# First attention unit: merged key and query loads, a split first decay load, half-size scaling and score passes, and a new queue order

## The chip, the cores and the metric

One Trainium2 chip, one of its cores. The metric is the device time of one launch in microseconds (us), lower is better; each figure is the median of several runs, and the profile is of one further execution.

## The reference

Four sequences of 768 steps and eight heads of width 48 run through a decayed linear attention; its output, 3072 tokens of width 384, goes through two feed-forward layers.

```python
for t in range(S):
    state = alpha[:, :, t, :, None] * state + einsum('bhd,bhe->bhde', k[:, :, t], v[:, :, t])
    y[:, :, t] = einsum('bhd,bhde->bhe', q[:, :, t], state)
...
h = x @ w_in;  x = (h * cos(h)) @ w_out                                   # 384 -> 2048 -> 384
h = maximum(maximum(x @ w1, x @ w2), x @ w3);  return h @ w_out           # 384 -> 768 -> 384
```

## The kernel before

The tokens are cut into 6 units of 512 columns (4 sequences of 128 steps). A unit's attention is done for pairs of heads, on 128 partitions; the first layer then takes 16 steps per unit (`moe1`: L763 to L765 into the hidden block, L794 to L796 out of it), 96 steps in all; the second layer (L1147 to L1149, L1056 to L1058) follows. The attention of units 1 to 5 (`prepare`, `turn`, `visit`) is slipped between the steps of the unit before. All weights of the first layer arrive once as 64-bit numbers, in 32 blocks (`weight`): a load (L386), an upper part on ScalarE (L387), a merge on VectorE (L388), a high half on ScalarE (L392) and a low half on GpSimd (L396) or VectorE (L394).

Unit 0 has nothing to hide behind; it is `first_unit`. Three wide head pairs k = 0, 1, 2 carry a fourth one in their spare partitions. For each k:

- `load0` (L445) issues the loads, all on SyncE's queue: decays `al` (128 rows of 522 numbers), keys and queries `kq` in two loads of 512 numbers a row, then the values `v` and `rest`.
- `chain0` (L461): VectorE forms backward products of the decays in two scans (L471), each over two sequences; GpSimd multiplies the keys by them (L473); ScalarE makes a copy of the scaled keys for the shared fourth pair (L474); VectorE forms the forward products (two reciprocals L477, two scans L478); GpSimd multiplies the queries by these (L480).
- `scores0` (L489) and `shared_scores0` (L501) are passes of 8 small matmuls on TensorE (16 in the trace: a float32 matmul counts twice), `mask0` (L435) takes a score block out of PSUM through VectorE, `values0` (L517) and `shared_values0` (L526) multiply by the values, `transposes0` (L547) and `state0` (L567) form the state for unit 1, `outputs0` hands unit 0 to `moe1`.

The order on every queue comes from a planner in the kernel (`Program.order`): each operation has an engine, a cost, a due time and what it reads and writes; a simulated clock picks, for the engine that is free first, the ready operation with the smallest due time. The numbers at the head of the file (`W1E` sets how early a weight block is due, `LATE` and `LATE_S` the transposes and states of unit 0, `ATT0`, `VIS` and their like the visits, `B_START` and `B_STEP` the weights of the second layer) are due times or offsets of such. What waits for what on the chip is set by semaphores, so the planner's clock decides only the order.

```python
for n, (key, f, b) in enumerate((alpha(0), keys(0, 0), alpha(1), keys(0, 1), keys(1, 0), alpha(2), keys(1, 1), keys(2, 0), keys(2, 1), vals(0), vals(1), vals(2), shared_vals())):
    op("SP", HW, f, (), [key], -40 + 0.1 * n, 0.95 * dma(b) if n else 0)
```

Of the kernel before, what the change touches and what calls it, by code (L numbers as in the profile page):

```python
# [60 lines left out]
B_START, B_STEP = 17.76, 2.27  # L61
# [8 lines left out]
GLE1, GLQ = 0, 15  # L70
GLP1 = 0
# [7 lines left out]
GATE, GSTEP = 0, 3  # L79
LGATE = 11  # L80
W0 = -0.9
LATE, LATE_S = -3.58, -4.98
LOD = (1, 3)

W1E = 21
MOE_EARLY = 5
EARLY = 3
FIRST = -4
ATT0 = 3.97
ATTS = 3.25  # L90
# [189 lines left out]
SLOW = 1.2  # L280
# [16 lines left out]
def tile_kernel(ctx, tc, aa, qk, vv, vr, wt, outT):  # L297
# [147 lines left out]
    def load0():  # L445
        def alpha(k):
            return ("inf", k), lambda: nc.sync.dma_start(al_f[k], aa[0, k, :, 0:KO]), P * KO * 4

        def keys(k, h):
            return ("inq" if h else "ink", k), lambda: nc.sync.dma_start(kq_f[k][:, HB * h:HB * (h + 1)], qk[0, k, :, HB * h:HB * (h + 1)]), P * HB * 4  # L450

        def vals(k):
            return ("v", k), lambda: nc.sync.dma_start(v_b[k], vv[0, k]), P * HB * 3

        def shared_vals():
            return "vr", lambda: nc.sync.dma_start(rest, vr.rearrange("p (i j k e) -> p i j k e", i=N2, j=2, e=32)), P * N2 * 2 * NT0 * 128

        for n, (key, f, b) in enumerate((alpha(0), keys(0, 0), alpha(1), keys(0, 1), keys(1, 0), alpha(2), keys(1, 1), keys(2, 0), keys(2, 1), vals(0), vals(1), vals(2), shared_vals())):
            op("SP", HW, f, (), [key], -40 + 0.1 * n, 0.95 * dma(b) if n else 0)

    def chain0(k):  # L461
        t, gf, kg = al_f[k], g_f[k % NGS], ("g", k % NGS)
        g = gf[:, 0:AP].rearrange("p (c t) -> p c t", c=N2)
        fv = t[:, 0:AP].rearrange("p (c t) -> p c t", c=N2)
        kv3, qv3 = views0(k)
        kf, kk, kq, ka = ("inf", k), ("ink", k), ("inq", k), ("acc", 2)
        t0 = -30 + k
        ones, seeds = acc[2][:, 0:AP // 2], acc[2][:, HB - AP // 2:][:, ::-1]
        for h in range(2):
            hs = slice(AP // 2 * h, AP // 2 * (h + 1))  # L470
            op("DVE", 0.07 + 0.00208 * AP / 2, lambda hs=hs: ve.tensor_tensor_scan(  # L471
                gf[:, 0:AP][:, ::-1][:, hs], t[:, 1:AP + 1][:, ::-1][:, hs], ones, 0.0, ALU.mult, ALU.add), [ka, kf, *([("scan", k - 1)] if k else [])], [(*kg, h)], t0)
        op("Pool", pool(HB), lambda: ge.tensor_tensor(kv3, kv3, g[:, :, 1:], ALU.mult), [(*kg, 0), (*kg, 1)], [kk], t0)  # L473
        op("Act", act(HB), lambda: se.activation(kr_b[k], kq_f[k][:, 0:HB], AF.Copy, scale=shared), [kk, "shared"], [krk[k]], t0)  # L474
        for h in range(2):
            hs, cs = slice(AP // 2 * h, AP // 2 * (h + 1)), slice(N2 // 2 * h, N2 // 2 * (h + 1))
            op("DVE", 0.15, lambda cs=cs: ve.reciprocal(seeds[:, ::CP], g[:, cs, 0]), [ka, (*kg, 1 - h)], ["seeds"], t0)  # L477
            op("DVE", 0.07 + 0.00208 * AP / 2, lambda hs=hs: ve.tensor_tensor_scan(  # L478
                t[:, hs], t[:, hs], seeds, 0.0, ALU.mult, ALU.add), [ka, "seeds", (*kg, 0), (*kg, 1)], [kf, ("scan", k)], t0)
        op("Pool", pool(HB), lambda: ge.tensor_tensor(qv3, qv3, fv[:, :, 1:], ALU.mult), [kf], [kq], t0)  # L480

    def scores0(k, n, t):
        rk, r = psum2("r0")
        kv3, qv3 = views0(k)

        def amm():
            for i in range(N2):
# [3 lines left out]
        op("PE", SLOW * 0.95, amm, [("ink", k), ("inq", k)], rk, t, tiled=True, count=32)  # L491
        return mask0(n, r, rk, t + 0.01)

    def shared_scores0(n, t):
        rk, r = psum2("r0")

        def amm(k):
            kr3, qv3 = kr_b[k].rearrange("p (c t) -> p c t", c=N2), views0(k)[1]
            for i in range(N2):
                for j in range(2):  # L500
                    pe.matmul(r[j][:, i * P:(i + 1) * P], kr3[wide_half[j], i], qv3[wide_half[j], i],  # L501
                              start=(not k and not i), stop=(k == NT0 - 1), skip_group_check=True)
# [38 lines left out]
    def transposes0(k, t):  # L541
# [7 lines left out]
        op("PE", SLOW * N2 * 0.085, trans, [("ink", k), "ident", ("y1", LGATE)], [pk_k], t, count=2 * N2)  # L549
# [56 lines left out]
    def prepare(n, t0):  # L606
# [8 lines left out]
        op("SP", HW, lambda: nc.sync.dma_start(al_f[na], aa[u, p, :, 0:KO]), (), [kf], t0 - 4.8 + (0.8 if not k else 0), dma(PR * KO * 4), tiled=True)  # L615
        op("SP", HW, lambda: nc.sync.dma_start(kq_f[nk], qk[u, p]), (), [kk, kq], t0 - 3.9, dma(PR * 2 * HB * 4), tiled=True)
# [819 lines left out]
```

## Time and profile before

| what | us |
|---|---|
| median of 3 runs | 739.33 (738.73 to 739.82) |
| the profiled execution | 738.83 |
| its span, first to last instruction | 736.9 |
| TensorE busy | 730.0, 99% of the span |
| VectorE, ScalarE, GpSimd busy | 539.7, 420.1, 303.8 |
| DMA, share of 16 engines | 47.4% |

The engines are named PE (TensorE), DVE (VectorE), ACT (ScalarE), POOL (GpSimd), SP (SyncE, which issues the loads). The ends of matmuls are modelled, so a group's length is best read from its start to the start of the next group. The clock that was granted to TensorE is 1.00 of full speed in every slice.

### The profile page before, as it was taken

How to read it: one execution, taken by the hardware profiler on the slowest of the kernel's cores; microseconds unless marked ns; L12 is line 12 of the kernel's file. 1: busy time of each engine (PE TensorE's matmuls, PEld its weight loads, DVE VectorE, ACT ScalarE, POOL GpSimd, SP SyncE). 2: the span in 40 equal slices, each digit the busy share in tenths (PEclk: the TensorE clock that was granted, in tenths of full speed). 3: DMA queues.
4: the chain of work that ended last, by engine and by line, in shares of the span. 5: the costliest groups of instructions: out<-in, count | busy, mean ns of one | idle time of the engine just before them, and what ended most of it. 6: DMA issues, size and time to landing. Idle time of an engine off the chain costs nothing.

```text
span 736.9 us, 14861 instructions
## 1 busy us (share of the span) xinstructions
PE 730.0 (99%) x5815; PEld 600.8 (82%) x5815; DVE 539.7 (73%) x858; ACT 420.1 (57%) x801; POOL 303.8 (41%) x284
## 2 busy tenths in 40 slices
PE   8999999999999999999999999999999999999997
PEld 6788888888888888888888888888888888888886
DVE  7999996877877776865655666467787768677763
ACT  4888866666756666667644655443563345634233
POOL 6444433556533635454320211043465543614442
PEclk9999999999999999999999999999999999999999
DMA  8866534564644554554250111397625556246302
GB/s 319 298 226 212 171 126 134 176 222 158 206 139 154 187 181 136 184 180 148 98 207 0 44 43 44 140 368 292 213 103 201 198 177 205 77 149 206 130 1 85
DMA packets 47525, 120.41 MB, mean 163 GB/s; under 512 B 4736, under 2 KB 19968, under 8 KB 42464
## 3 DMA queue, kind: packets, MB, share of 16 engines
q1 hardware_dynamic: 47456, 119.48, 47.4%
q8 instruction: 45, 0.74, 0.4%
q14 instruction: 24, 0.20, 0.1%
HBM read 91.54 MB, written 25.95 MB: 159 GB/s over the span
## 4 chain that ended last, share of the span: by engine, by line
PE 96%; DVE 1%; ACT 1%; DMA 1%; issue 0%; SPq 0%; POOL 0%; DVEq 0%; POOLq 0%
PE acc L794 9%; PE ps L763 9%; PE acc L795 9%; PE acc L796 9%; PE ps L764 9%; PE ps L765 9%; PE ps L1147 6%; PE ps L1148 6%; PE ps L1149 6%; PE acc L1148 3%; PE acc L1147 3%; PE acc L1149 3%; PE acc L1057 2%; PE acc L1058 2%; PE acc L1056 2%; PE ps L662 2%
## 5 line engine op out<-in xcount | busy, mean ns | idle before, releaser
L763 PE MATMUL ps<-xt,wih 128*128 128x512 f32 x288 | 114.5, 397 | 0.0
L794 PE MATMUL acc<-gg,woh 128*128 128x512 f32 x288 | 114.4, 397 | 0.0
L796 PE MATMUL acc<-gg,woh 128*128 128x512 f32 x288 | 112.3, 390 | 0.2 <-DVE gg L789 0.2
L795 PE MATMUL acc<-gg,wol 128*128 128x512 f32 x288 | 112.2, 390 | 0.0
L764 PE MATMUL ps<-xt,wih 128*128 128x512 f32 x288 | 112.2, 390 | 0.0
L765 PE MATMUL ps<-xt,wil 128*128 128x512 f32 x288 | 112.2, 389 | 0.0
L772 DVE SCALAR_TENSOR_TENSOR q<-q,ps 128x512 f32<-128x512 int32 x96 | 65.5, 683 | 39.7 <-ACT q L771 39.2
L773 ACT ACTIVATE q<-q 128x512 f32<-128x512 f32 x96 | 60.4, 631 | 39.4 <-DVE q L772 39.2
L777 DVE TENSOR_TENSOR gg<-q,gg 128x512 fp32r<-128x512 f32 x81 | 62.8, 779 | 23.2 <-ACT gg L776 22.6
L771 ACT ACTIVATE q<-ps 128x512 int32<-128x512 f32 x96 | 56.9, 593 | 39.4 <-PE ps L765 37.4
L775 DVE TENSOR_TENSOR q<-q,ps 128x512 f32<-128x512 f32 x81 | 55.2, 681 | 33.0 <-ACT q L773 32.3
L776 ACT ACTIVATE gg<-q 128x512 fp32r<-128x512 f32 x81 | 51.1, 631 | 35.5 <-DVE q L775 31.1
L937 POOL TENSOR_TENSOR ar<-ar,ar 128x512 f32<-128x512 f32 x21 | 28.6, 1365 | 92.1 <-DVE as L946 67.8
L796 PEld LDWEIGHTS acc<-gg,woh 128*128 128x128 f32 x288 | 54.1, 188 | 12.1 <-DVE gg L789 0.8
L794 PEld LDWEIGHTS acc<-gg,woh 128*128 128x128 f32 x288 | 54.0, 188 | 11.8
L765 PEld LDWEIGHTS ps<-xt,wil 128*128 128x128 f32 x288 | 54.1, 188 | 11.3
L763 PEld LDWEIGHTS ps<-xt,wih 128*128 128x128 f32 x288 | 54.1, 188 | 11.1
L795 PEld LDWEIGHTS acc<-gg,wol 128*128 128x128 f32 x288 | 54.1, 188 | 10.4
L764 PEld LDWEIGHTS ps<-xt,wih 128*128 128x128 f32 x288 | 54.1, 188 | 10.4
L1155 ACT ACTIVATE q<-acc 128x512 f32<-128x512 f32 x36 | 21.5, 597 | 69.2 <-PE acc L1149 68.5
L1166 POOL TENSOR_TENSOR xf<-q 128x512 f32<-128x512 f32 x18 | 24.5, 1364 | 81.4 <-ACT q L1155 81.4
L1019 ACT ACTIVATE fs<-x 128x512 fp32r<-128x512 f32 x42 | 26.2, 630 | 44.8 <-DVE x L1170 30.0
(187 smaller groups left out, 1727.1 us busy)
## 6 DMA issues: line engine op xcount, KB each, us to landing
bs<-bfd SPq DMA_DIRECT2D x36, 1024.0 KB, 5.0
raw<-in_wt SPq DMA_DIRECT2D x56, 384.0 KB, 3.9
bfd<-bs SPq DMA_DIRECT2D x32, 384.0 KB, 2.9
kq<-in_qk SPq DMA_DIRECT2D x20, 512.0 KB, 4.4
al<-in_aa SPq DMA_DIRECT2D x23, 261.0 KB, 2.8
x1r<-yy SPq DMA_DIRECT2D x18, 256.0 KB, 2.1
ar<-x1r SPq DMA_DIRECT2D x18, 256.0 KB, 2.9
v<-in_vv SPq DMA_DIRECT2D x23, 192.0 KB, 4.5
```

The costliest lines, as they stand in the source:

```text
L763: pe.matmul(ps, wi["h"][:, f, cc], xt[:, cc, 0], start=(cc == 0), stop=False)
L764: pe.matmul(ps, wi["h"][:, f, cc], xt[:, cc, 1], start=False, stop=False)
L765: pe.matmul(ps, wi["l"][:, f, cc], xt[:, cc, 0], start=False, stop=(cc == NR - 1))
L772: op("DVE", dve(HB), lambda: ve.scalar_tensor_tensor(q, q.bitcast(I32), -TWOPI, ps, ALU.mult, ALU.add), [hk], [qk], m)
L773: op("Act", act(HB), lambda: se.activation(q, q, AF.Sin, bias=0.5 * math.pi), (), [qk], m)
L777: op("DVE", dve(HB), lambda: ve.tensor_tensor(gl, q, gh.bitcast(F32), ALU.subtract), [qk, ("gh", gn)], [("gl", gn)], m, port=True)
L794: pe.matmul(acc[c], oh, gh, start=(f == 0), stop=False)
L795: pe.matmul(acc[c], ol, gh, start=False, stop=False)
L796: pe.matmul(acc[c], oh, gl, start=False, stop=(f == NF1 - 1))
L1147: pe.matmul(bank, bt[:, i, 0], at[:, 0], start=start, stop=False, skip_group_check=skip)
L1148: pe.matmul(bank, bt[:, i, 0], at[:, 1], start=False, stop=False, skip_group_check=skip)
L1149: pe.matmul(bank, bt[:, i, 1], at[:, 0], start=False, stop=stop, skip_group_check=skip)
```

## The change

`load0` loads keys and queries of a pair in one transfer, and the first decays in two (columns 258 to 521 first, then 0 to 257). `chain0` scales the keys of pair 0 and the queries of all three pairs in halves of two sequences, and each score pass of the unit is cut into two halves that wait for their half alone. The numbers that set due times are new, and `GLP1` gives the low half of step 0 of the first layer to GpSimd.

```diff
-B_START, B_STEP = 17.76, 2.27
+B_START, B_STEP = 31.64, 2.16
...
-GLE1, GLQ = 0, 15
-GLP1 = 0
+GLE1, GLQ = 0, 16
+GLP1 = 1
...
-GATE, GSTEP = 0, 3
-LGATE = 11
+GATE, GSTEP = 1, 0
+LGATE = 14
...
-LATE, LATE_S = -3.58, -4.98
+LATE, LATE_S = -4.18, -2.37
...
-W1E = 21
-MOE_EARLY = 5
+W1E = 37
+MOE_EARLY = 6
...
-ATT0 = 3.97
-ATTS = 3.25
-VIS, VEND, VQ = 3.95, 12, 0.98
-LARGE, STALL, PATIENT = 2, -0.53, 2.75
-V2, V2S, TA = 16.24, 2.98, 0.97
+HALF_K, HALF_Q, SPLIT0 = (0,), (0, 1, 2), True
+ATT0 = 4.42
+ATTS = 1.66
+VIS, VEND, VQ = 4.24, 13, 0.53
+LARGE, STALL, PATIENT = 2, -1.22, 8.27
+V2, V2S, TA = 17.49, 2.63, 1.77
...
-SLOW = 1.2
+SLOW = 1.06
...
+        def keys(k):
+            return [("ink", k), ("inq", k)], lambda: nc.sync.dma_start(kq_f[k], qk[0, k])
...
+        first = [(0.1, 0.0, [("infb", 0)], alpha(0, cut, KO)), (0.4, 0.0, [("inf", 0)], alpha(0, 0, cut))] if SPLIT0 else [(HW, 0.0, [("inf", 0)], alpha(0))]
...
+        if k in HALF_K:
+            for h in (1, 0):
+                cs = halves0[h][1]
+                op("Pool", pool(HB // 2), lambda cs=cs: ge.tensor_tensor(kv3[:, cs], kv3[:, cs], g[:, cs, 1:], ALU.mult), [(*kg, 1 - h), kk], [("kp", k, h)], t0)
...
-        op("Pool", pool(HB), lambda: ge.tensor_tensor(qv3, qv3, fv[:, :, 1:], ALU.mult), [kf], [kq], t0)
+        if k in HALF_Q:
+            for h in range(2):
+                cs = halves0[h][1]
+                op("Pool", pool(HB // 2), lambda cs=cs: ge.tensor_tensor(qv3[:, cs], qv3[:, cs], fv[:, cs, 1:], ALU.mult), [("f0", k, h), kq], [("qp", k, h)], t0)
...
+    def score_parts(k, go, keys, rk, t):
+        parts = ((0, 1), (2, 3)) if k in HALF_Q else ((0, 1, 2, 3),)
+        for p in parts:
+            hs = sorted({i // 2 for i in p})
+            op("PE", SLOW * 0.95 * len(p) / 4, lambda p=p: go(p), [*(x for h in hs for x in (*keys(h), *queries0(k, h)))], rk, t, tiled=True, count=8 * len(p))
```

What that does to the order stands below, at three places. In the names, `al_124` to `al_126` are the decays of pairs 0 to 2, `kq_104` to `kq_106` their keys and queries, `g_127` and `g_128` backward products of pairs 0 and 1, `raw_88` to `raw_91` four buffers of weight blocks, `inv_122` a buffer that is zeroed for unit 1.

SP's queue from the first load, before:

```order
L447 DMA al_124<-in_aa 128x522
L450 DMA kq_104<-in_qk 128x512
L447 DMA al_125<-in_aa 128x522
L450 DMA kq_104<-in_qk 128x512
L450 DMA kq_105<-in_qk 128x512
```

and in the changed kernel:

```order
L450 DMA al_124<-in_aa 128x264
L387 DMA raw_88<-in_wt 128x1536
L450 DMA al_124<-in_aa 128x258
L453 DMA kq_104<-in_qk 128x1024
L450 DMA al_125<-in_aa 128x522
L453 DMA kq_105<-in_qk 128x1024
```

A weight block (128 rows of 1536 two-byte numbers) now goes second, between the two parts of the first decays; before, the first weight block was behind all 13 loads of the unit.

POOL from its first product, before:

```order
L473 TENSOR_TENSOR kq_104<-kq_104,g_127 128x512
L480 TENSOR_TENSOR kq_104<-kq_104,al_124 128x512
L473 TENSOR_TENSOR kq_105<-kq_105,g_128 128x512
L480 TENSOR_TENSOR kq_105<-kq_105,al_125 128x512
```

and in the changed kernel:

```order
L480 TENSOR_TENSOR kq_104<-kq_104,g_127 128x256 x2
L493 TENSOR_TENSOR kq_104<-kq_104,al_124 128x256 x2
L483 TENSOR_TENSOR kq_105<-kq_105,g_128 128x512
L397 TENSOR_TENSOR wil<-raw_88,wih 128x384
L493 TENSOR_TENSOR kq_105<-kq_105,al_125 128x256
L630 MEMSET inv_122 112x520
L493 TENSOR_TENSOR kq_105<-kq_105,al_125 128x256
```

The low half of the first weight block now stands between the keys and the queries of pair 1, and a zeroing between the halves of these queries.

DVE from the backward products of pair 1, before:

```order
L471 SCALAR_TENSOR_TENSOR g_128<-al_125,acc_98 128x258 x2
L477 RECIPROCAL acc_98<-g_128 128x2
L478 SCALAR_TENSOR_TENSOR al_125<-al_125,acc_98 128x258
```

and in the changed kernel:

```order
L474 SCALAR_TENSOR_TENSOR g_128<-al_125,acc_98 128x258 x2
L389 SCALAR_TENSOR_TENSOR raw_88<-raw_88,top_92 128x384
L487 RECIPROCAL acc_98<-g_128 128x2
L488 SCALAR_TENSOR_TENSOR al_125<-al_125,acc_98 128x258
```

The merge of the first weight block now comes ahead of the forward products of pair 1; before it stood behind all scans of the unit.

## Rows read from the trace of the kernel before

**Rows 1.** The page: busy time by engine, share of the span, instructions.

```profile
PE 730.0 (99%) x5815; PEld 600.8 (82%) x5815; DVE 539.7 (73%) x858; ACT 420.1 (57%) x801; POOL 303.8 (41%) x284
```

**Rows 2.** Busy time by stretches: length, PE, PEld, DVE, ACT, POOL, clock, DMA share, GB/s.

```profile
0.00:5.00 5.00, 3.57 (x10) 2.54 (x11) 3.29 (x10) 1.89 (x4) 2.18 (x16) 1.00 0.57 162
5.00:10.00 5.00, 3.62 (x40) 2.99 (x40) 4.76 (x11) 1.96 (x4) 3.66 (x4) 1.00 0.97 336
10.00:15.00 5.00, 4.96 (x80) 4.05 (x79) 4.93 (x11) 2.39 (x5) 4.30 (x5) 1.00 1.05 406
...
700.00:737.00 37.00, 33.17 (x147) 27.13 (x145) 20.06 (x26) 14.45 (x25) 14.14 (x10) 1.00 0.12 43
```

**Rows 3.** Who PE waited for, whole span: total us, times, longest.

```profile
PE acc L1257 <- POOL ident masks.py:199: 1.4, 1, 1.4
PE ps L489 <- POOL kq L480: 1.4, 1, 1.4
PE acc L796 <- DVE gg L789: 0.2, 1, 0.2
```

**Rows 4.** PE in order of time: start, length, what, idle before and its releaser.

```profile
6.36 0.66 PE L547 MATMUL ps<-ident,kq 128*128 128x128 f32 x4
8.40 1.16 PE L489 MATMUL ps<-kq 48*128 48x128 f32 x16 [1.39 <-POOL kq L480]
...
10.38 0.66 PE L547 MATMUL ps<-ident,kq 128*128 128x128 f32 x4
11.08 1.16 PE L501 MATMUL ps<-kq,inv 64*128 64x128 f32 x16
...
22.77 0.66 PE L547 MATMUL ps<-ident,kq 128*128 128x128 f32 x4
23.18 0.48 PE L763 MATMUL ps<-xt,wih 128*128 128x512 f32 x1
23.50 0.39 PE L764 MATMUL ps<-xt,wih 128*128 128x512 f32 x1
23.73 0.40 PE L765 MATMUL ps<-xt,wil 128*128 128x512 f32 x1
...
31.37 0.40 PE L795 MATMUL acc<-gg,wol 128*128 128x512 f32 x1
31.93 0.50 PE L796 MATMUL acc<-gg,woh 128*128 128x512 f32 x1 [0.16 <-DVE gg L789]
```

**Rows 5.** POOL in order of time.

```profile
7.17 1.17 POOL L480 TENSOR_TENSOR kq<-kq,al 128x512 f32<-128x512 f32 x1 [0.87 <-DMA kq<-in_qk]
8.30 1.19 POOL L473 TENSOR_TENSOR kq<-kq,g 128x512 f32<-128x512 f32 x1
9.84 1.18 POOL L480 TENSOR_TENSOR kq<-kq,al 128x512 f32<-128x512 f32 x1 [0.35 <-DVE al L478]
...
16.09 1.02 POOL L396 TENSOR_TENSOR wil<-raw,wih 128x384 fp32r<-128x384 f32 x1 [1.12 <-DMA raw<-in_wt]
...
22.48 1.19 POOL L623 TENSOR_TENSOR kq<-kq,g 112x512 f32<-112x512 f32 x1
```

**Rows 6.** The chain of waits: start, length, what.

```profile
2.18 4.83 DMA kq<-in_qk
```

**Rows 7.** Busy time by stretches, as in rows 2, for the DMA columns.

```profile
3.50:4.00 0.50, 0.50 (x4) 0.50 (x3) 0.41 (x1) 0.00 (x0) 0.00 (x0) 1.00 0.65 157
...
5.00:6.00 1.00, 1.00 (x7) 0.97 (x6) 0.93 (x3) 0.00 (x0) 0.88 (x1) 1.00 0.99 314
11.00:12.00 1.00, 0.96 (x17) 0.92 (x18) 1.00 (x3) 0.77 (x2) 1.00 (x3) 1.00 1.04 412
```

**Rows 8.** DVE in order of time.

```profile
3.59 1.27 DVE L471 TENSOR_TENSOR_SCAN g<-al,acc 128x258 f32<-128x258 f32 x2 [0.44 <-DMA al<-in_aa]
...
14.85 0.56 DVE L388 SCALAR_TENSOR_TENSOR raw<-raw,top 128x384 uint32<-128x384 uint32 x1
...
22.77 1.32 DVE L388 SCALAR_TENSOR_TENSOR ps<-raw,top 128x384 uint32<-128x384 uint32 x1
```

More of the change, by code (lines that the diff above doesn't have):

```diff
@@ L445, in load0, with alpha @@
     def load0():
[L446 to L450, printed above, removed]
-        def vals(k):
[L453 to L459, printed above, removed]
+        cut = AP // 2
+        def alpha(k, lo=0, hi=KO):
+            return lambda: nc.sync.dma_start(al_f[k][:, lo:hi], aa[0, k, :, lo:hi])
+        def keys(k):
+            return [("ink", k), ("inq", k)], lambda: nc.sync.dma_start(kq_f[k], qk[0, k])
+        def vals(k):
+            return [("v", k)], lambda: nc.sync.dma_start(v_b[k], vv[0, k])
+        shared_vals = [("vr")], lambda: nc.sync.dma_start(rest, vr.rearrange("p (i j k e) -> p i j k e", i=N2, j=2, e=32))
+        first = [(0.1, 0.0, [("infb", 0)], alpha(0, cut, KO)), (0.4, 0.0, [("inf", 0)], alpha(0, 0, cut))] if SPLIT0 else [(HW, 0.0, [("inf", 0)], alpha(0))]
+        for n, (w, us, keys_, f) in enumerate((*first, (HW + (0.4 if SPLIT0 else 0.0), 0.55 if SPLIT0 else 0.93, *keys(0)), (HW, 1.4, [("inf", 1)], alpha(1)), (HW, 1.2, *keys(1)),
+                                        (HW, 0.8, [("inf", 2)], alpha(2)), (HW, 1.3, *keys(2)), *((HW, 0.5, *vals(k)) for k in range(3)), (HW, 1.0, *shared_vals))):
+            op("SP", w, f, (), keys_, -40 + 0.1 * n, us * RATE)
     def chain0(k):
@@ L468, in chain0 @@
         ones, seeds = acc[2][:, 0:AP // 2], acc[2][:, HB - AP // 2:][:, ::-1]
-        for h in range(2):
-            hs = slice(AP // 2 * h, AP // 2 * (h + 1))
+        halves0 = [(slice(AP // 2 * h, AP // 2 * (h + 1)), slice(N2 // 2 * h, N2 // 2 * (h + 1))) for h in range(2)]
+        for h, (hs, _) in enumerate(halves0):
             op("DVE", 0.07 + 0.00208 * AP / 2, lambda hs=hs: ve.tensor_tensor_scan(
-                gf[:, 0:AP][:, ::-1][:, hs], t[:, 1:AP + 1][:, ::-1][:, hs], ones, 0.0, ALU.mult, ALU.add), [ka, kf, *([("scan", k - 1)] if k else [])], [(*kg, h)], t0)
@@ L473, in chain0 @@
[L473 to L476, printed above, removed]
+                gf[:, 0:AP][:, ::-1][:, hs], t[:, 1:AP + 1][:, ::-1][:, hs], ones, 0.0, ALU.mult, ALU.add),
+               [ka, *([kf] if k or h or not SPLIT0 else []), *([("infb", 0)] if SPLIT0 and not k else []), *([("scan", k - 1)] if k else [])], [(*kg, h)], t0)
@@ new lines, in chain0 @@
+        if k in HALF_K:
+            for h in (1, 0):
+                cs = halves0[h][1]
+                op("Pool", pool(HB // 2), lambda cs=cs: ge.tensor_tensor(kv3[:, cs], kv3[:, cs], g[:, cs, 1:], ALU.mult), [(*kg, 1 - h), kk], [("kp", k, h)], t0)
+            kks = [("kp", k, 0), ("kp", k, 1)]
+        else:
+            op("Pool", pool(HB), lambda: ge.tensor_tensor(kv3, kv3, g[:, :, 1:], ALU.mult), [(*kg, 0), (*kg, 1)], [kk], t0)
+            kks = []
+        op("Act", act(HB), lambda: se.activation(kr_b[k], kq_f[k][:, 0:HB], AF.Copy, scale=shared), [kk, *kks, "shared"], [krk[k], *([("kz", k)])], t0)
@@ new lines, in chain0, with keys0, queries0 @@
+        if k in HALF_Q:
+            for h in range(2):
+                cs = halves0[h][1]
+                op("Pool", pool(HB // 2), lambda cs=cs: ge.tensor_tensor(qv3[:, cs], qv3[:, cs], fv[:, cs, 1:], ALU.mult), [("f0", k, h), kq], [("qp", k, h)], t0)
+        else:
+            op("Pool", pool(HB), lambda: ge.tensor_tensor(qv3, qv3, fv[:, :, 1:], ALU.mult), [kf], [kq], t0)
+    def keys0(k, h):
+        return [("ink", k), *([("kp", k, h)] if k in HALF_K else [])]
+    def queries0(k, h):
+        return [("inq", k), *([("qp", k, h)] if k in HALF_Q else [])]
@@ L484, in scores0, with amm @@
         kv3, qv3 = views0(k)
-        def amm():
-            for i in range(N2):
+        def amm(p):
+            for i in p:
                 for j in range(2):
                     pe.matmul(r[j][:, i * P:(i + 1) * P], kv3[half[j], i], qv3[half[j], i], start=True, stop=True)
-        op("PE", SLOW * 0.95, amm, [("ink", k), ("inq", k)], rk, t, tiled=True, count=32)
+        score_parts(k, amm, lambda h: keys0(k, h), rk, t)
         return mask0(n, r, rk, t + 0.01)
@@ L495, in shared_scores0, with amm @@
         rk, r = psum2("r0")
-        def amm(k):
+        def amm(k, p):
             kr3, qv3 = kr_b[k].rearrange("p (c t) -> p c t", c=N2), views0(k)[1]
-            for i in range(N2):
+            for i in p:
                 for j in range(2):
```

13 lines of the change are left out of this document (8 added, 5 removed).

## Prediction

> **What bounds the kernel now.** I read the page first: TensorE is busy 730.0 of 736.9 us [rows 1]. Then the busy time by stretches: of the 6.9 us without TensorE, 3.83 lie behind the last matmul (37.00 less 33.17), 1.43 before the first and 1.38 in the stretch from 5 to 10 us; from 10 to 15 us it is already 4.96 of 5.00 [rows 2]. The list of waits agrees: 1.4 for `ident`, 1.4 at L489 for GpSimd's L480, 0.2 at L796 [rows 3]. So the kernel is one long stream of matmuls behind a start of 8.4 us, and the change can earn only in its start.
>
> Since ends are modelled, I read the start from start to start [rows 4]. The same four transposes (L547) are followed 0.41 later at 22.77, but 2.04 later at 6.36 and 0.70 later at 10.38. TensorE thus waits 1.63 before the first score pass at 8.40 and 0.29 before 11.08, both times for GpSimd's L480, which ends at 7.17 + 1.17 = 8.34 and 9.84 + 1.18 = 11.02 [rows 5]. Later, L796 follows L795 after 0.56 where its like take 0.23 (23.50 to 23.73): 0.33 of waiting for a low half from VectorE [rows 4]. Together 2.25 us can be won: even without any of it the profiled 738.83 would be 736.58. I call "faster" and "slower" what goes beyond 0.2%, 1.48 us, about what measurements of this kernel can tell from no change; faster needs two thirds of all waits.
>
> Why is L480 late? GpSimd sat idle 0.87 until the queries landed [rows 5], at 2.18 + 4.83 = 7.01 in the chain [rows 6]. The first decays were there at 3.59 [rows 8]. The start is bound by loads, then by GpSimd.
>
> **Term 1: the first score pass.** By the shapes (rows x numbers x bytes), 1058 kB were ahead of the end of the first queries (267 + 262 + 267 + 262). Now 1184 kB are ahead of the merged load's end: 135 of decays, 393 of the weight block that slipped in second, 132 of decays, 524 of keys and queries. The first decay part should land near 3.59 less 132 kB at 314 GB/s [rows 7], 3.17. For the other 1049 kB the trace gives three paces: 231 GB/s, as from 3.59 to 7.01 (791 kB in 3.42 us); 314, as from 5 to 6 us with rows of 2 kB; and 412, as from 11 to 12 us with rows of 1.5 and 3 kB [rows 7]. Landing: 7.7 at the slowest, 5.7 at the fastest. I take 6.1: 917 kB in rows of 3 and 4 kB at 412 (2.23), 132 kB at 314 (0.42), and 0.3 for the lull of 157 GB/s at 3.5 to 4.0 us [rows 7], which I see no reason to be gone (0.5 us at under half the pace). GpSimd begins 0.16 after the landing (7.17 to 7.01) and makes three halves before the first half pass can run: both of the keys, one of the queries. A half is not in the trace: from half of 1.19 (0.60) to a straight line through 512 and 384 columns (1.19 and 1.02 [rows 5]), 0.85 at 256; I take 0.68, nearer to the half since these rows' lengths are almost proportional. So: 6.1 + 0.16 + 2.04 + 0.06 (8.34 to 8.40) = 8.36, against 8.40: **-0.04**, between -0.7 and +2.1. The weight block's 393 kB cost 0.95 at 412, which is what the smaller passes and the merged load earn. The second half of the queries is ready at 9.0, long before TensorE asks for it, and nothing is gained from half passes beyond the first: four of them take the 1.98 that two whole ones did (8.40 to 10.38).
>
> **Term 2: waits inside the unit.** The 0.29 before 11.08 goes, because the new order puts other work there: transposes of pair 1 at 10.34 (8.36 + 1.98), then a state pass and the values of pair 0. These need what was not urgent before. (a) The state pass needs the first values: 1779 kB behind the queries, 4.3 us at 412, 5.7 at 314, so 10.5 to 11.9, where TensorE stands at 10.75 (10.34 + 0.41): 0 to 1.0, taken as 0.2, most of it being 4 kB rows. (b) The values of pair 0 need two masks on VectorE; the weight merge (0.56, L388 at 14.85 [rows 8]) is now ahead of them: 0 to 0.5, taken as 0. (c) The shared values need masks that stand behind weight work: 0 to 0.6, taken as 0.2. (d) GpSimd's low half of the block (1.02) and a zeroing stand before the second half of pair 1's queries; with keys of pair 1 done at 10.4 that half is done near 13.4, and TensorE, by then busy with states and values, asks at 14: nothing. If that cover went (values early), it would cost up to 1. Sum -0.29 + 0.4 = **+0.11**, between -0.3 and +1.8.
>
> **Term 3: more changes between small and wide matmuls.** By the order of TensorE's instructions the unit now goes from one to the other three times more, the rest once less. One costs 0.09 (23.18 to 23.50 against 0.23 [rows 4]), up to 0.11 on the way back: **+0.2**.
>
> **Term 4: the first steps of the first layer.** The 0.33 at L796 is for a low half that VectorE makes; GpSimd makes it now. The states of unit 0 and the first turn come before the steps instead of among them, so nothing else is changed in the amount of TensorE's work. From 0 to -0.33, taken as **-0.15**. The visits, the other weights and the second layer's weights (which start 14 steps later) move on engines that TensorE does not wait for: 5.00 of 5.00, or 4.96, from 10 us on [rows 2]. Their cover is the stock of blocks made ahead; if it runs dry, each step waits for a block.
>
> **Sum.** -0.04 + 0.11 + 0.2 - 0.15 = +0.12, so 738.95 for the profiled execution. That execution (738.83) lies 0.5 below the median of the runs shown; on the median, 739.33 + 0.12, **739.5 us**.
>
> **The rivals.**
>
> *Gain.* Large rows keep the fast pace from the first block on, no lull: landing at 5.7, halves of 0.62, first pass at 7.8 (-0.6), no waits (-0.29), the step wait gone (-0.33), changes +0.2: -1.0, 738.3. For it: 404 to 412 GB/s wherever rows are large. Against it: the lull at the start. Beyond 1.48 only if the weight block also costs nothing.
>
> *Slower: the weight block holds up everything behind it.* If the queue goes on as from 3.59 to 7.01, the queries land at 7.1 or after (7.7 at that pace to the end); with halves of 0.75 the first pass is then at 9.6. From there the unit slides as a whole, since TensorE is full behind it: +1.2 at the first pass, +0.5 in waits (values later too), +0.2: +1.9, 741.2. It decides from a landing of about 7 on. For it: 231 GB/s is what the trace shows for exactly these microseconds. Against it: it was 2 kB rows.
>
> *Slower: merge and products block each other.* L388 took 1.32 at 22.77 instead of 0.56 at 14.85 [rows 8]; GpSimd ran L623 from 22.48 to 23.67 [rows 5], and L388 ended 0.42 after it, as if it had begun then. The moved merge runs among GpSimd's half products and can be held until one ends, 0.3 to 1.2, and with it pair 1's scans, masks and the values of pair 0: +0.9 on the sum, 740.4. The Trainium skill states it as a rule (SBUF — State Buffer, section "Who interferes with whom"): a VectorE instruction with two SBUF inputs and a GpSimd instruction that reads SBUF exclude each other, and the one that started first keeps the shared ports to its end. By that rule the time is 740.4 whenever a product has begun before the merge; the pair at 22.77 agrees with it.
>
> *The change doesn't do what it says.* The first pass is earlier by nothing, as in my sum; that case is the forecast itself.
>
> The Trainium skill (DMA: Bandwidth & Descriptors, section "Bandwidth") advises loads of 1 MiB or more. By it the merged load (0.5 MiB) should be better than two of half the size, and the split decays worse; by its fit in "Anatomy of one DMA" (436 GB/s once moving) the landing would come out at 5.6, an estimate, and the sum near -0.4. The 231 to 314 GB/s of the rows here are below it, and they decide.
>
> **Chances.** Forecast 0.50 (738.8 to 740.3); gain 0.20, of which 0.07 beyond 1.48; blocked load 0.18, of which 0.15 beyond; merge 0.12, of which 0.06 beyond. Faster 0.07, slower 0.21, the same 0.72. The range reaches to the gain's 738.3 and the blocked load's 741.2.
>
> **What would show it.** Right: keys and queries of pair 0 landing near 6.1; the first score pass between 8.0 and 8.7; small waits of PE for values and masks between 10.5 and 12 and near 19; no wait over 0.5 later. Wrong: a first pass before 7.8 or after 9.3, a merge of over 1 us on VectorE before 11 us, or waits of PE after 30 us that sum to over 0.7; any of these moves the time by its own length.

## The result, and the profile after

The changed kernel takes 742.63 us (median of 7 runs, 741.41 to 746.02) against 739.33 before (738.58 to 739.87): 1.0051 times as long, with an interval of 1.0038 to 1.0064. The profiled execution took 743.52 with a span of 740.6, where before had 738.83 and 736.9; 1.0 of its 4.7 us lies outside the span. The runs lie 4.6 us apart, those of before 1.3. The two longest (745.69 and 746.02) had a mean granted clock of 0.995 and 0.997, the other five 0.999 or 1.000.

The page, busy time by engine, and the list of PE's waits:

```profile
PE 731.2 (99%) x5815; PEld 601.5 (81%) x5815; DVE 539.0 (73%) x857; ACT 422.2 (57%) x801; POOL 307.4 (42%) x289
```

```profile
PE ps L577 <- POOL kq L480: 3.2, 1, 3.2
PE acc L1287 <- POOL ident masks.py:199: 1.4, 1, 1.4
PE acc L824 <- ACT yy L833: 0.4, 1, 0.4
```

TensorE's lines have moved by 30: L577 is L547 of before, L519 is L489, L531 is L501, L793 to L795 are L763 to L765. GpSimd's lines moved otherwise: L480 is now the product of the keys (L473 before), L493 that of the queries (L480 before). The wait of [rows 3] for `ident` is the same, and the one for the first products has grown from 1.4 to 3.2. Busy time by stretches (columns as in [rows 2]):

```profile
5.00:10.00 5.00, 1.83 (x11) 1.40 (x10) 3.39 (x7) 0.53 (x2) 1.50 (x3) 1.00 0.97 348
10.00:15.00 5.00, 5.00 (x76) 4.27 (x78) 4.32 (x10) 3.48 (x8) 5.00 (x7) 1.00 1.04 403
```

TensorE has lost 1.79 us of work between 5 and 10 us (3.62 to 1.83), at a full clock and with the DMA engines busy. PE in order of time, then POOL, then one row of the chain of waits, to be read against [rows 4], [rows 5] and [rows 6]:

```profile
9.88 0.65 PE L577 MATMUL ps<-ident,kq 128*128 128x128 f32 x4 [3.17 <-POOL kq L480]
10.47 0.71 PE L519 MATMUL ps<-kq 48*128 48x128 f32 x8
...
27.65 0.50 PE L793 MATMUL ps<-xt,wih 128*128 128x512 f32 x1
...
342.41 0.39 PE L795 MATMUL ps<-xt,wil 128*128 128x512 f32 x1
343.17 0.50 PE L824 MATMUL acc<-gg,woh 128*128 128x512 f32 x1 [0.37 <-ACT yy L833]
```

```profile
8.50 1.32 POOL L480 TENSOR_TENSOR kq<-kq,g 128x256 f32<-128x256 f32 x2 [5.20 <-DMA kq<-in_qk]
9.78 1.64 POOL L493 TENSOR_TENSOR kq<-kq,al 128x256 f32<-128x256 f32 x2
```

```profile
2.19 6.15 DMA kq<-in_qk
```

The keys with queries were issued at 2.19 and over at 8.34; GpSimd began its first half 0.16 later, and the first score pass started at 10.47 instead of 8.40. That is 2.07 of the 3.7 us by which the span grew. The rest needs a sum. I read four more parts from start to start:

- The unit, from the first score pass to the first projection: 17.18 (10.47 to 27.65). Before it was 14.78 (8.40 to 23.18), to which belong 0.86 for two state passes (24.75 to 25.61) and 0.47 for a turn (transposes for unit 1, 30.56 to 31.03) that stood behind the first projections there: 16.11. So +1.07.
- Two waits of before, between the first steps, are gone: 0.33 before L796 [rows 4] and 0.28 of the same kind behind L765 at 34.80. Together -0.61.
- Gaps of over 0.14 more than usual behind 36 us: before one of 0.20, now 0.20 (64 us), 0.53 (342 us) and 0.24 (574 us): +0.77.
- From the end of the last addition on DVE to the end of the span: 2.93 before (733.97 to 736.9), 3.42 now (737.18 to 740.6): +0.49.

Together 3.79, against 3.7 measured. The lines for these parts, three stretches of PE and the last addition from before, then the last addition now:

```profile
24.75 0.56 PE L567 MATMUL ps<-v,bw 128*48 128x48 f32 x16
25.15 0.53 PE L567 MATMUL ps<-yy,kt 128*48 128x48 f32 x16
25.61 0.50 PE L763 MATMUL ps<-xt,wih 128*128 128x512 f32 x1
...
30.56 0.55 PE L636 MATMUL ps<-ident,kq 112*128 112x112 f32 x4
31.03 0.50 PE L794 MATMUL acc<-gg,woh 128*128 128x512 f32 x1
...
34.80 0.39 PE L765 MATMUL ps<-xt,wil 128*128 128x512 f32 x1
35.30 0.69 PE L662 MATMUL ps<-kq 48*64 48x64 f32 x32
...
733.28 0.69 DVE L1074 TENSOR_TENSOR xf<-ps,xf 128x512 f32<-128x512 f32 x1
```

```profile
736.49 0.69 DVE L1104 TENSOR_TENSOR xf<-ps,xf 128x512 f32<-128x512 f32 x1
```

### The profile page after: what moved, and what is told of

It is laid out like the page before. It is cut to its first block, busy times and chain, and to the rows that moved or that the text cites. A ratio compares the mean times of both kernels' runs of the same rounds, so it can differ in the third digit from the quotient of the medians.

```text
span 740.6 us, 14890 instructions
## 1 busy us (share of the span) xinstructions
PE 731.2 (99%) x5815; PEld 601.5 (81%) x5815; DVE 539.0 (73%) x857; ACT 422.2 (57%) x801; POOL 307.4 (42%) x289
## 4 chain that ended last, share of the span: by engine, by line
PE 97%; DVE 1%; DMA 1%; ACT 0%; issue 0%; SPq 0%; POOL 0%; POOLq 0%; DVEq 0%; ACTq 0%
PE ps L793 9%; PE acc L824 9%; PE ps L794 9%; PE ps L795 9%; PE acc L826 9%; PE acc L825 9%; PE ps L1177 6%; PE ps L1179 5%; PE ps L1178 5%; PE acc L1177 3%; PE acc L1179 3%; PE acc L1178 3%; PE acc L1086 2%; PE acc L1088 2%; PE acc L1087 2%; PE ps L692 2%
## 5 line engine op out<-in xcount | busy, mean ns | idle before, releaser
L793 PE MATMUL ps<-xt,wih 128*128 128x512 f32 x288 | 114.6, 398 | 0.0
L824 PE MATMUL acc<-gg,woh 128*128 128x512 f32 x288 | 114.2, 396 | 0.4 <-ACT yy L833 0.4
L795 PE MATMUL ps<-xt,wil 128*128 128x512 f32 x288 | 112.2, 390 | 0.0
L807 DVE TENSOR_TENSOR gg<-q,gg 128x512 fp32r<-128x512 f32 x80 | 60.7, 761 | 26.5 <-ACT gg L806 26.1
L824 PEld LDWEIGHTS acc<-gg,woh 128*128 128x128 f32 x288 | 54.0, 188 | 12.2 <-ACT yy L833 0.8
L793 PEld LDWEIGHTS ps<-xt,wih 128*128 128x128 f32 x288 | 54.1, 188 | 11.5 <-issue 0.2
L795 PEld LDWEIGHTS ps<-xt,wil 128*128 128x128 f32 x288 | 54.1, 188 | 11.4
L1177 PE MATMUL ps<-as,bs 128*128 128x512 f32 x126 | 49.4, 392 | 0.1
```

The costliest lines, as they stand in the source:

```text
L793: pe.matmul(ps, wi["h"][:, f, cc], xt[:, cc, 0], start=(cc == 0), stop=False)
L795: pe.matmul(ps, wi["l"][:, f, cc], xt[:, cc, 0], start=False, stop=(cc == NR - 1))
L807: op("DVE", dve(HB), lambda: ve.tensor_tensor(gl, q, gh.bitcast(F32), ALU.subtract), [qk, ("gh", gn)], [("gl", gn)], m, port=True)
L824: pe.matmul(acc[c], oh, gh, start=(f == 0), stop=False)
L1177: pe.matmul(bank, bt[:, i, 0], at[:, 0], start=start, stop=False, skip_group_check=skip)
```

## Experiments

"Before" is here the kernel before, run beside each experiment on its chip (medians 739.17 to 739.37); the number after each range is the time as a multiple of before's, with a 95% interval. Three theories stood first: **A**, the weight block ahead of the queries makes them late; **B**, a merged load is over only when the slowest of the 16 DMA engines is, so one big load is worse than two; **C**, the new order's waits inside the unit cost, and the landing is not all.

**1. The block behind the queries.** In the list of planned operations, the order otherwise untouched:

```diff
+    loads = [i for i in order if G.ops[i][0] == "SP"]
+    order.remove(loads[1])
+    order.insert(order.index(loads[3]) + 1, loads[1])
```

> The changed kernel with one move on SP's queue: the weight block that goes second is issued fourth, behind both parts of the first decays and the first keys and queries; every other engine's order is the same. Theory A (the block ahead of the queries is what made them land at 8.33 instead of about 6): kq0 lands 1 to 2 us earlier, 6.3 to 7.3, the first score pass comes at 8.4 to 9.4 instead of 10.47, and the time falls by 1 to 2, to 740.6 to 741.6. Theory B (the merged load waits for the slowest of 16 DMA engines, whatever is ahead): the spread of its 16 landings stays near 2.5 us, the first pass gains less than 0.5, the time stays above 742. Theory C (the loss is waits that the new order makes inside the unit): within 0.4 of the changed kernel.

Measured: 741.51 (739.94 to 742.97), 1.0029 [1.0019, 1.0039]. First score pass at 8.45, 2.0 earlier, but only 1.1 came back. PE in order of time shows what took the rest:

```profile
8.45 0.72 PE L519 MATMUL ps<-kq 48*128 48x128 f32 x8
...
10.80 0.66 PE L577 MATMUL ps<-ident,kq 128*128 128x128 f32 x4 [0.30 <-POOL kq L483]
11.88 0.56 PE L597 MATMUL ps<-v,bw 128*48 128x48 f32 x16 [0.42 <-DVE a L436]
```

The transposes of pair 1 waited 0.37 and the state pass 0.50 (572 and 698 ns from start to start, where 202 is usual at these two changes of shape); the first values landed at 11.75, just ahead of L597. In the changed kernel these waits are hidden behind the larger one. So A fits the first pass, and C what remains; but of the 2.0 a part is the chance of one execution (experiments 13 and 14).

**2. Keys and queries apart.** `keys(k)` issues two loads of 512 numbers instead of one of 1024.

> The changed kernel with keys and queries of each pair again in two loads, issued one behind the other at the same place of the queue; all else the same. Theory A: the bytes ahead of the last query are the same, the first pass stays within 0.4 of 10.47 and the time within 0.4 of 742.6. Theory B: the products of the keys start when the keys are there, about 1 us before the queries, so the first pass comes 0.6 to 1.3 earlier and the time is 741.3 to 742.0. Theory C: no change.

Measured: 742.21 (741.99 to 742.39), 1.0039 [1.0026, 1.0052]. Keys landed at 6.60, queries at 7.24, first pass 8.74, but the state pass now waits 0.5 for the values' DMA. Against the profiled execution the first pass is 1.7 earlier, as B has it; but in three further executions with the one load it stood at 8.47 to 8.97 (experiments 13 to 15), so B isn't shown, and the time hardly moved.

**3 and 4. Code and numbers apart.** The changed code with all numbers of before (`W1E = 21`, `HALF_K, HALF_Q, SPLIT0` as in the change, the others as before), and the code of before with all new numbers.

> The changed code (merged loads, split first decays, half products and passes) with all planner numbers of the kernel before; no weight block ahead of the unit's loads, and the transposes, states and weights in about the old places. Theory A: the queries land at 6 to 6.8, the first pass comes at 8.0 to 8.8, the time is 739.0 to 740.0. Theory B: queries still past 7.3, first pass past 9.3, time 740.2 to 741. Theory C: like before, 739.0 to 739.6.

> The kernel before with the new planner numbers: its own 13 loads, but the weight block second on the queue, and the new order of weights, transposes and visits. Theory A: first queries land 1 to 2 later than 7.01, first pass at 9.4 to 10.4, time 740.4 to 741.4. Theory B: landing like before, time 739.2 to 739.7. Theory C: +1 from waits inside the unit whatever the landing, 740.3 to 741.5, with PE waits of values and masks that add up to about 1.

Measured: 743.42 (740.55 to 744.40), 1.0050 [1.0035, 1.0065], and 754.06 (753.77 to 756.60), 1.0208 [1.0194, 1.0222]. The first has its queries at 5.22 and its first pass at 7.37, 1.0 earlier than before, and still is 4 us slower. Its waits of PE:

```profile
PE ps L531 <- POOL kq L493: 1.1, 1, 1.1
PE ps L717 <- issue: 1.1, 1, 1.1
PE ps L666 <- DVE wol L395: 0.8, 1, 0.8
```

The one of L717 is at 250 us, that of L666 at 49. The second kernel has four waits of 0.8 to 1.8 between 49 and 342 us. An early start alone bought nothing here, and neither the code nor the numbers do well without the other.

**5 and 6. The block behind the whole unit, with its work on ACT, DVE and POOL.** Then the same with half passes side by side and one copy at 342 us earlier:

```diff
+    moved([loads[1]], loads[11])
+    moved([nth("Act", 388), nth("DVE", 389), nth("Act", 393), nth("Pool", 397), loads[17]], nth("DVE", 436, 3))
```

> After, with the first weight block put wholly behind the unit: its load stands behind the values of the three pairs and the shared values, and its chain on ACT, DVE and POOL (L388, L389, L393, L397) behind the masks of the second pair; nothing else is moved. Theory Q (all that is lost before 27 us is bytes ahead in the load queue and the chain of that block): keys with queries of pair 0 land as in the run with the block behind the queries (last of 16 at 6.3), but the first decays of pair 1, pair 1's keys and the values of pair 0 land about 0.9 us earlier than there (a 393 KB load at the pace of that run), so the two waits at 9.88 to 10.80 (0.47) and 10.80 to 11.88 (0.50) vanish; the first L793 starts at 25.0 to 25.3 instead of 26.05 and the time is about 740.5. Theory H (size changes and the new order inside the unit): the waits shrink but L519 and L531 keep their surplus over before of 0.2 to 0.7 in sum, first L793 25.5 or later, time 741.0 to 741.5. Theory L (late waits): whatever the start, the 0.5 at 342 us stays, and the time lies 1.5 or more over the kernel before.

> The kernel of the run with the block behind the unit, with two more edits: the two half passes of a score pass stand one behind the other (third pass behind the first in pair 0, and so on), so that fewer changes of shape are left, and the third copy of finished outputs near 342 us (L833 on ACT) stands one L779 earlier. Theory H: the surplus of L519 and L531 falls by 0.2 to 0.4, the first L793 by the same; theory L: the gap of 759 ns at 342.4 between L795 and L824 falls to about 300, and both together bring 0.6 to 0.9 against the run without them, to 739.6 to 739.9. Theory Q: neither brings anything that can be measured, because only the queue counted. If it comes below 739.0 it beats the kernel before.

Measured: 743.75 (743.51 to 744.45), 1.0059 [1.0047, 1.0071], and 745.24 (742.96 to 745.73), 1.0074 [1.0061, 1.0088]: the wrong way. The second pair's pass did come earlier (12.60 against 13.25 in experiment 1), and both waits there were gone; but at 20 us a new one stood, since the block's work that had been moved (and the next block's L388 behind it) was now ahead of a copy on ACT:

```profile
PE ps L519 <- ACT kt L583: 1.2, 1, 1.2
```

```profile
19.43 0.55 ACT L393 ACTIVATE wih<-raw 128x384 fp32r<-128x384 f32 x1 [0.21 <-DVE raw L389]
19.89 0.63 ACT L388 ACTIVATE top<-raw 128x384 f16<-128x384 bf16 x1
20.38 0.26 ACT L583 ACTIVATE kt<-ps 128x128 f32<-128x128 f32 x1
```

The second kernel can't be read for its passes: moving a half pass made the program put a filler matmul of 1.06 us ahead of another (at 16.27), and L519 and L531 take 6.35 in both. It also had a wait "issue" of 1.0 at 121 us. What it did show: with the copy earlier the gap at 342 us is gone.

**7. The load queue of the kernel before, swapped.** Queries of pair 0 ahead of the first decays of pair 1.

> The kernel before, with one edit: on the load queue the queries of pair 0 stand ahead of the first decays of pair 1 (third and fourth load swapped). Theory: the first score pass sets the time one for one (what the landing costs or saves is paid in full): queries land about 0.6 us earlier (6.4 instead of 7.0), the first score pass starts at 7.6 to 7.8 instead of 8.40 and the time falls by 0.6, to 738.7. Rival: the second pair sets it: its score pass at 11.08 waits for POOL's product of pair 1, which waits for decays that land 0.6 later; the first pass comes earlier, the second at 11.1 to 11.6, and the time is the same or up to 0.5 longer, 739.3 to 739.8.

Measured: 739.29 (738.44 to 740.68, 11 runs), 0.9999 [0.9990, 1.0007]. Queries at 6.55, first pass at 8.19, and the second pair waits instead:

```profile
8.19 1.16 PE L489 MATMUL ps<-kq 48*128 48x128 f32 x16
9.18 1.06 PE L501 MATMUL ps<-kq,inv 64*128 64x128 f32 x16
10.17 0.66 PE L547 MATMUL ps<-ident,kq 128*128 128x128 f32 x4
11.74 0.94 PE L501 MATMUL ps<-kq,inv 64*128 64x128 f32 x12 [0.91 <-POOL kq L480]
```

In the kernel before, then, an earlier first pass bought nothing, as the second pair's products set the pass behind it. The swap itself made them later (the decays of pair 1 landed at 7.26 instead of 6.37), so what an earlier first pass alone would be worth isn't shown.

**8. Fillers in the start wait.** Eight filler matmuls more ahead of the first transposes of the changed kernel.

> After, with 8 more filler matmuls (they write a bank that nothing reads) ahead of the first transposes, so that PE is busy for most of the wait of 3.5 us from 6.3 to 9.9. Theory: the two runs of after at 745.7 and 746.0 (granted clock 0.995 and 0.997) come from that wait, PE's clock being granted lower for some time behind it: with the filler no run lies above 743.5, and the median falls to about 742. Rival: the wait itself is all that is lost: the median stays at 742.6 and the scatter too. First score pass at 10.4 to 10.6 by both.

Measured: 747.37 (746.83 to 749.74), 1.0113 [1.0098, 1.0128]. I had sized it wrong: the eight took 6.87 (7.36 to 14.23) instead of some 2.6, so nothing can be said of the scatter. The first score pass stood at 14.76 instead of 10.47, 4.29 later, and the median was 4.74 longer than the changed kernel's. That is near to a start paid in full, but it doesn't price it: the profiled execution took 749.74, with late gaps of about 3.2 of its own, and the first passes of the runs in the changed kernel's median aren't known.

**9. A longer program on POOL.** Before, with 18 memsets of 16 numbers at 440 us:

```diff
+            if i == late:
+                for _ in range(18):
+                    ge.memset(scratch[0:16, 0:1], 0.0)
```

> The kernel before with 18 more instructions on POOL: memsets of 16 by 1 on a pad that nothing reads, at 440 us, where POOL is mostly idle. After has 457 records on POOL, before 439, and every kernel of the study with 450 or fewer ends 2.9 to 3.0 us behind the start of its last tail addition's end, those with 457 or more 3.4 to 3.5, with an 8 KB packet of the instruction queue and a POOL DRAIN of 220 ns instead of 78 there. Theory (POOL must fetch one more block of its program at the very end): this kernel has the late packet, the stretch from the end of the last DVE addition to the end of the span is 3.4 instead of 2.93, and the time is 0.3 to 0.5 longer, 739.6 to 739.9. Rival (the longer end has to do with the new order or the output transfer): no late packet, 2.9, same time as before.

Measured: 739.70 (739.12 to 740.78, 11 runs), 1.0006 [0.9997, 1.0014]; last addition to end 3.33 instead of 2.93. DMA queues from 736 us on, in this kernel, where before has no packet at all:

```profile
q1 hardware_dynamic: 62, 0.09, 4.2%
q14 instruction: 1, 0.01, 0.5%
```

GpSimd's last but one DRAIN took 221 ns in the trace, as in the changed kernel (220), against 78 before. Both programs have 457 records on POOL, before 439. The 0.4 to 0.5 at the end is shown in the trace; in the time, whose interval holds 1, it isn't. (The 62 packets are the end of the output's transfer, which in the kernel before was over by 736.)

**10. The block back, finer.** As the second of 5 and 6, with the block's work put into gaps of ACT, DVE and POOL one by one, and L583 next to its L580.

> The kernel with the block behind the unit, whole passes and the earlier copy, with the chain of that block put into gaps: L388 behind the first state copy on ACT, L389 behind the last first decays on DVE, L393 behind the shared keys of pair 2, L397 behind the last product on POOL, and the copy L583 of pair 2 next to its L580. Theory Q (the chain that was moved made the new wait of 0.8 to 1.2 us at 20 us, nothing else is wrong with the block put back): the wait of L519 on ACT is gone or under 0.3, the first L793 starts at 26.0 to 26.4 (27.22 in both runs with the block put back whole), and the time falls by about 1 against the kernel with the block behind the unit, to 742.5 or less. Rival (the start is not what sets these kernels, late waits with releaser issue do): the start improves so, and the time stays at 743.5 to 745.

Measured: 742.21 (741.43 to 742.34), 1.0038 [1.0026, 1.0050]. The wait on ACT is gone and behind 36 us only 0.49 is left, the time fell by 1.5 against 5; but the first L793 is at 27.88, not 26.0 to 26.4: the same filler of 1.06 stands there (at 17.06), and 0.83 of "issue" before L531 at 16.42. So neither expectation fits whole. Q holds for the wait at 20 us; but as the first L793 is 0.7 later than in 5 (27.22), the 1.5 came from behind it: past 36 us about 0.5 of late gaps stands against over 2 in the kernel of 5.

**11. The new numbers without halves**, `HALF_K, HALF_Q, SPLIT0 = (), (), False`, planned anew.

> After with its numbers and its load of keys with queries, but with the first decays in one load and without the halves (whole products, whole passes); the order is planned anew from that. Theory of the landing: the raw block stays ahead of the keys, the first pass needs a whole key product (1.2) instead of two halves and a whole query product behind it, so it starts about 1.2 us later than where the halves are, at 11 to 12, and the time is that of after plus 0.5 to 1.5. Theory of the halves (they cost more in changes of shape than they bring): the surplus of L519 and L531 (0.64 in sum) goes away, and the time is equal to that of after or up to 0.6 below it, 742.0 to 742.6.

Measured: 743.60 (741.47 to 745.19), 1.0057 [1.0041, 1.0073]. First pass at 9.30 after a landing at 6.76; waits of 0.73 at 32, 0.85 at 46, 0.53 at 342 and 0.47 at 571 us more than usual. Neither theory's number. The surplus of L519 and L531 did fall, from 0.64 to 0.15, and the unit took 0.33 more than before's (15.97 against 14.78 and 0.86) instead of 1.07: the halves cost TensorE about 0.5 in the unit. The waits that the new plan has further on took that back, so the time doesn't show it.

**12. The block late, planned anew**, `W1E = 21` alone.

> After with the one number that puts the weight blocks' due time to that of before (21 instead of 37), everything planned anew from that. Theory (the block ahead of the keys is what costs): keys with queries land at about 6.0 to 6.4, the first score pass starts at 8.3 to 8.6, and the time is 741 or less. Rival (a plan whose numbers were found together loses more late than it gains at the start): the first pass starts so, and the time is 742 or more, with waits behind 30 us that after does not have.

Measured: 740.90 (740.16 to 741.40, 11 runs), 1.0021 [1.0012, 1.0030]. Queries at 5.34, first pass 7.96, first L793 24.54: the start of before (23.18, with the 1.33 that stood behind it there 24.51), and the best of all changed kernels.

```profile
7.96 1.16 PE L519 MATMUL ps<-kq 48*128 48x128 f32 x16
...
24.54 0.50 PE L793 MATMUL ps<-xt,wih 128*128 128x512 f32 x1
```

The time that the theory of the block gave, 741 or less, is met: of the 3.3 us by which the change is slower, 1.7 went with this one number. As the plan is a new one, that isn't the landing's price alone. Its three longest waits behind the first pass are at 19, 31 and 341 us:

```profile
PE ps L519 <- ACT s L601: 0.8, 1, 0.8
PE ps L793 <- DVE q L809: 0.4, 1, 0.4
PE acc L824 <- ACT yy L833: 0.4, 1, 0.4
```

**13 and 14. The changed kernel itself, two more executions (a and b).** Unchanged.

> The changed kernel once more, one profiled execution. Theory (chance): the last of the 16 parts of keys with queries lands late in some executions and not in others, as in five executions of kernels whose first three loads are alike (6.30, 6.33, 5.31, 5.28, 5.34): it lands between 6.6 and 7.4 here, the first score pass starts at 8.7 to 9.5, and the time is 741 to 742. Theory (rule): the weight block ahead of it makes the landing late every time: 8.0 or later, first pass at 10.2 or later, 742.5 or more.

> The same kernel and the same two theories as in the other look: landing 6.6 to 7.4 and first pass 8.7 to 9.5 by chance, 8.0 or later and 10.2 or later by rule; if the two looks differ by over 0.5 us in the landing, the time of each should differ by the same amount.

Measured: 744.41 and 741.10. Execution a has its landing at 6.82 and its first pass at 8.97, b 6.32 and 8.47. A line of a, then one of b:

```profile
8.97 0.72 PE L519 MATMUL ps<-kq 48*128 48x128 f32 x8
```

```profile
7.88 0.66 PE L577 MATMUL ps<-ident,kq 128*128 128x128 f32 x4 [0.53 <-POOL kq L480]
```

So 8.33 was that one execution's chance, not a rule. But the time didn't follow: a, with a first pass 1.5 earlier than the profiled execution's, took 0.9 longer, and a and b, 0.5 apart in the landing, lie 3.3 apart. The longest waits of PE in a:

```profile
PE acc L826 <- issue: 0.7, 1, 0.7
PE ps L577 <- POOL kq L480: 0.7, 1, 0.7
PE ps L597 <- DMA v<-in_vv: 0.5, 1, 0.5
PE acc L824 <- ACT gg L806: 0.3, 1, 0.3
```

The sum of the result's section, for the three executions of the same program (us against before; late gaps are those of over 0.14 behind 36 us):

| part | profiled | execution a | execution b |
|---|---|---|---|
| first score pass (8.40) | +2.07 | +0.57 | +0.07 |
| unit, first pass to first L793 (16.11) | +1.07 | +1.40 | +1.01 |
| the two step waits of before | -0.61 | -0.61 | -0.61 |
| late gaps (0.20) | +0.77 | +2.39 | +1.20 |
| last addition to the end (2.93) | +0.49 | +0.51 | +0.50 |
| sum; span measured | 3.79; 3.7 | 4.26; 4.7 | 2.17; 2.2 |

**15. The copy at 342 us one place earlier**, in the changed kernel.

> After with one edit: the third copy of finished outputs near 342 us (L833 on ACT) stands one L779 earlier. Theory (the wait of 759 ns between L795 and L824 at 342.4 is paid in full): that gap falls to 250 to 350 ns and the time by 0.4 to 0.5, to 742.1 or 742.2. Rival (behind it the next wait takes up what it leaves): the gap falls and the time stays at 742.6.

Measured: 741.63 (740.75 to 743.92, 9 runs), 1.0031 [1.0020, 1.0041], 1.0 below the changed kernel's median. From L795 to L824 at 342 us it is now 0.23 instead of 0.76, so the gap is gone; the one wait of L824 that is left, 0.2, is at 261 us. The size isn't settled: the changed kernel's own runs lie 4.6 us apart, and in this profile the first pass was at 8.49. No kernel of the study beats the one before.

## Why the prediction was wrong, point by point

**"Landing: 7.7 at the slowest, 5.7 at the fastest. I take 6.1" (term 1)** failed for the profiled execution, and not by its pace. Half of the load's 16 parts were there by 6.2, close to the 6.1; but a load is over with its last part, which came at 8.33, and at 6.82, 6.32 and 6.34 in other executions with the same queue, 7.14 in the one with fillers. All three of my paces were means over 16 engines. Experiments 1, 3, 5, 6, 10 and 12, which have no weight block among their first three loads, show such a scatter too: last part at 6.30, 5.22, 6.33, 5.31, 5.29, 5.34. With the earliest landing the term was right, 8.47 against my 8.36; with the middle one of the five (6.82) the first pass was at 8.97. A half product takes 0.65 to 0.66; I had 0.68, and up to 0.85 in the range, which is why +2.07 still lies inside the term's -0.7 to +2.1.

**"The weight block holds up everything behind it" (the rival)** had the right mechanism. With the block ahead the landings lie between 6.32 and 8.33 (five executions, middle 6.82), without it, issued 0.5 earlier, between 5.22 and 6.33 (six, middle 5.33): about 1.5, where I had given the block's bytes 0.95. Its point, a landing of 7, was passed in the profiled execution. But b, with a landing of 6.32, still was 1.9 slower than before (741.10 against 739.17), and experiment 12, with a first pass earlier than before's, 1.7: the block isn't the whole cause.

**Terms 2 and 3, +0.31 together**, measured +1.01 to +1.40. The -0.29 in it was misread: behind four transposes a small pass starts 0.59 later when nothing is waited for (12.62 to 13.20 and 18.40 to 18.99 in the changed kernel), not 0.41, so before waited 0.11 at 11.08 and 1.45 at 8.40, and 1.9 rather than 2.25 could be won. The values waited as far as (a) said: 0.5 in a, 0.1 in b. (b) and (c) didn't appear in the profiled execution. What was mis-sized is term 3: L489 and L501 took 5.95 for their 96 matmuls, L519 and L531 take 6.59, and the state passes 2.02 instead of 1.74: 0.92 where I had 0.2 for net two changes. Three more gaps of 0.2 where 0.1 is usual make 0.3 of it, as priced; a gap of 0.28 behind a state pass (where 0.14 is usual) is another part, and the rest I can't assign. What is left to 1.07 lies in the transposes, the turn and the values, under 0.08 in each.

**Term 4, -0.15**, was too small on the good side: the 0.33 is gone, and so is a second wait of 0.28 at 34.80, which I hadn't seen.

**"Move on engines that TensorE does not wait for"** is the largest miss in a and b; in the profiled execution the landing was the larger miss. I read PE full behind 10 us and took the new order there as free. Behind 36 us 0.77, 1.20 and 2.39 were lost in three executions of one program, some of it in the same places (0.53 at 342 us in two, 0.24 to 0.34 near 574 in all), some not. Experiment 15 shows for the one at 342 us that the order makes it. Of a's 2.39, though, 1.35 (0.92 at 121 us, 0.43 at 341) are waits for blocks of TensorE's own program (last section), so the order's share is 0.8 to 1.2. Three executions of the old order (before, experiments 7 and 9) had 0.2, at most 0.2 and 0.7 of such gaps in all. My own sign for being wrong, waits behind 30 us that sum to over 0.7, is met in each. A full engine shows that the old order hides everything, not that another one will.

**No term at all** stood for the end of the program: +0.5.

**"Merge and products block each other"**: the changed kernel's merge and the product beside it on POOL.

```profile
10.22 0.62 DVE L389 SCALAR_TENSOR_TENSOR raw<-raw,top 128x384 uint32<-128x384 uint32 x1
```

The merge took 0.62 against 0.56 [rows 8], so here the rival fell as I priced it. But GpSimd's two halves from 9.78 on took 1.64 instead of 1.33, so the second was late by about 0.3, ending at 11.42, just ahead of the pass at 11.47; no pass waited for it. In b the merge met other products and took 0.98 (8.54 to 9.52). POOL there:

```profile
7.78 1.33 POOL L493 TENSOR_TENSOR kq<-kq,al 128x256 f32<-128x256 f32 x2
9.06 1.50 POOL L483 TENSOR_TENSOR kq<-kq,g 128x512 f32<-128x512 f32 x1
```

The merge began while L493 ran and ended 0.41 behind that one's end (9.11), as at 22.77 before [rows 8]; the keys of pair 1 then took 1.50 instead of 1.18 (1.38 in a), and the transposes, which wait for them, came about 0.2 later in both. So the rival was there, at 0.2 instead of its 0.9. All this agrees with the Trainium skill's rule (SBUF — State Buffer, "Who interferes with whom") that whoever starts first holds the ports, in b first GpSimd and then DVE.

**"Gain"** came nearest to the truth at the start: in experiments 10 and 12 the first pass stood at 7.99 and 7.96, nearly as early as its 7.8, and the times stayed above before's. As experiment 7 shows, the second pair's products stand behind it.

What stays open: what makes single DMA parts late, why the granted clock was lower in some runs, and why 1.0 us more lay outside the span in the profiled execution than before, but only 0.1 more in b. The waits "issue" (0.7 in a, 1.1 and 1.0 in experiments 3 and 6) are traced in the last section to blocks of TensorE's own program; why those blocks came late is open too.

## What to carry to other kernels

Price a load that everything waits for by its slowest part, seen in several executions, and not by a mean pace. When a small edit makes a planner order a whole program anew, the order's new waits far behind the edit are a cost of their own, here 0.8 to 1.2 us, about half of all that the edit could win; so ask for the edit under the old order too, and look where the second stage waits before paying for an earlier first one.

## What the runs showed of the hardware

The 16 parts of one load, issued together at 2.19, landed between 5.84 and 8.33. In the other executions with the merged load the last part came 0.2 to 1.2 behind the middle one. The Trainium skill (DMA: Bandwidth & Descriptors, "Latency and other measured facts") gives an access to HBM 0.2 us on average and 2 under high load, which would be of this size; no run here shows that it is the cause.

The length of an engine's program reached the time at its very end. Kernels with 439 to 450 records on POOL ended 2.9 to 3.0 behind the last addition, those with 453 to 458 3.3 to 3.5, and 18 idle memsets moved the kernel before from the one group to the other. The packet that goes with it is on queue 14, which the Trainium skill (CRC Debugging, "Comparing the Two Runs") names as that of the sequencers' instruction refill; the trace agrees in calling it "instruction", as it does queue 8. In those it is stamped within 0.6 us of the span's end, so it marks the crossing and isn't itself what is waited for; the kernel with 450 records (experiment 4) had such a packet 1.5 us behind its span, and the short end.

TensorE's program shows in the waits "issue" too. Queue 8 brought 45 packets of 16 KB in a run, for 11,713 records of TensorE (5815 matmuls, as many weight loads, 83 others): one for about 256. A line of the page of the changed kernel, and the wait of execution a in its chain of waits:

```profile
q8 instruction: 45, 0.74, 0.4%
```

```profile
121.93 0.75 issue
```

The five longest such waits behind 36 us (0.26 to 1.09 us, in a and in experiments 3, 5, 6 and 8) end behind 2754, 5826, 2754, 2753 and 4291 records: each 193 to 195 past a multiple of 256. A packet of queue 8 ended 1.3 to 1.5 us before TensorE went on. Of the other crossings of that place in the 17 traces, all but two had their packet over 1.5 us ahead, most over 4. The two are a gap of 0.17 in experiment 9 and the 0.43 at 341 us in a, for which the profile names ACT. So TensorE waited in these for the next block of its program; the "issue" of experiment 10 at 16 us (behind 283 records) isn't of this kind.
